# Packing W1 and W2 into seven 64-row halves in a two-branch transformer block

## The chip, the cores and the metric

The kernel runs on one core of one Trainium2 chip. The metric is device time in microseconds (us); lower is better. A run with a profile also leaves a trace, and times inside the kernel are counted from the start of the traced span. All runs told of here are in the fast state, but for two of the four runs of experiment 2, which are marked where they come. The kernel before was run again beside the experiments, on several chips, with medians of 177.70 to 178.31 us in place of 177.94; so totals of different experiments compare only within some 0.6 us.

Engine names as the profile prints them: PE is TensorE's matmuls, PEld its weight loads, DVE is VectorE, ACT is ScalarE, POOL is GpSimd, SP is the sync engine, which here only issues DMAs.

## The reference

With S = 2048 tokens, D = 448, F = 1792 and 16 heads, on xn = layernorm(x):

```python
def _B_ref(x, w1, w2, w3, w4):                 # called with x = xn
    h  = gelu(layernorm(x) @ w1)                # 448 -> 448
    c  = D // 4                                 # 112 features in each quarter
    # quarter 0 takes token t-1, quarter 1 token t+1, quarter 2 token t-2, quarter 3 token t+2
    hs = concatenate([shift(h[:, :, k*c:(k+1)*c]) ...]) @ w2
    x1 = x + hs
    return x1 + gelu(layernorm(x1) @ w3) @ w4

out = x + attention(xn) + _B_ref(xn)            # attention: linear, with softmax feature maps of +p and -p
```

## The kernel before

Everything is bf16, sums are in PSUM, TensorE's result memory. The kernel uses its banks two at a time, as bank pairs. A recorder keeps the order in which operations are written, and each engine executes its own operations strictly in that order. The line numbers in the profile are the recorder's helpers, so groups are told apart by tile names: `xnT` and `gT` are transposed activations, `w` holds w1, w2, w3 and w4, `hT` is gelu(xn W1), `wpk` and `wpq` the folded weights of K and Q, `vaug` the V values, `phik` the key features, `g_tok` the second layernorm's output before its transpose.

K = 448 does not divide by 128. The kernel therefore works with pairs of 64-row matmuls: one on partitions 0 to 63 and one on 64 to 127, into different PSUM banks, run at the same time. Such a pair is called a pair-step below. For W2 it kept four chunks of 112 features, one for each shift, so a chunk is a 64-row half and a 48-row half:

```python
def w1_pair(g, m, b):            # 512 tokens x two chunks of 112 features
    return lap_pair([banks[2 * b + k][0:CR, :] for k in range(2)],
                 lambda k, kc, lo, hi: w1[lo:hi, kc, CR * (m + k):CR * (m + k) + CR],
                 lambda k, kc, lo, hi: xnT[lo:hi, kc, 512 * g:512 * g + 512])

def w2_pair(i, b):               # token tiles i and i + 1
    def side(k, lo, hi):
        r = []
        for m in range(NM):      # four chunks; the shift is a column offset
            c0 = 2 + 128 * (i + k) - SHIFTS[m]
            r.append((banks[2 * b + k][:, 0:D], hT[lo:hi, m, c0:c0 + 128], w2[lo:hi, m, :]))
        return r
    return (lambda: row_pairs(side(0, 0, 64), side(1, 64, CR), True),
            lambda: row_pairs(side(1, 0, 64), side(0, 64, CR)))
```

After the token and W1 stage come eight attention steps, each with a K pair, a Q pair and one W2 or V pair, and then the W3/W4 stage:

```python
side = [("w", 0), ("v", 12), ("w", 2), ("w", 4), ("v", 14), ("w", 6), ("w", 8), ("w", 10)]
g_at = {2: (0,), 3: (1,), 4: (2, 3), 6: (4,), 7: (5,)}
for ps in range(8):
    ...
    if kind == "w":
        w2_out(i, 2)             # DVE: xn += W2 result
    ...
    k_norm(2 * ps)               # DVE: sum, reciprocal; POOL: multiply phik, 3.2 us
    if kind == "w" and i < 8:
        w2_norm(i)               # DVE: statistics of tiles i, i+1; POOL: scale, every 4 tiles
    for t in g_at.get(ps, ()):
        g_apply(t)               # POOL: normalise tile t
        g_T(t)                   # SP: DMA transpose into gT
# ... [cut] ...
play([A(6, 7), G(6, 7), a(0), (wl[12][0],), b(0), ...   # a(0): first W3 pair, reads gT of tiles 0 to 3
```

The softmax here doesn't subtract the row's maximum and nothing guards it: scores larger than these inputs give would overflow.

## Time and profile before

| | before |
|---|---|
| median of 4 runs | 177.94 us (177.75 to 178.07) |
| TensorE matmul busy | 170.8 us of a span of 175.9 |
| attention steps start | 31.4 us |
| W3 stage starts | 69.0 us |

First the page of the kernel before: TensorE's busy line, its row and its clock's row in the 40 slices (tenths), and the chain that ended last, by engine.

```profile
PE 170.8 (97%) x2198; PEld 94.7 (54%) x2198; DVE 110.0 (63%) x252; ACT 82.5 (47%) x92; POOL 93.7 (53%) x130
...
PE   7899999998999999999999999999999999999993
...
PEclk9999999999999999999999999999999999999999
...
PE 91%; DVE 6%; issue 1%; POOL 0%; ACT 0%; DVEq 0%
```

TensorE is busy nearly everywhere, and 91% of the chain of waits lies on it: whatever delays TensorE is paid in full.

The windows view of the kernel before gives one line for each stage: length, then busy time (and instructions) of PE, PEld, DVE, ACT and POOL, the granted clock, the DMA share and GB/s.

```profile
core 0: us, PE busy (x) PEld busy (x) DVE busy (x) ACT busy (x) POOL busy (x), PEclk, DMA share, GB/s
0.00:17.70 17.70, 15.86 (x176) 10.48 (x178) 13.92 (x39) 9.71 (x14) 10.16 (x34) 1.00 0.81 205
17.70:31.40 13.70, 13.69 (x209) 8.84 (x206) 7.87 (x20) 9.49 (x13) 5.74 (x10) 1.00 0.56 142
31.40:69.00 37.60, 37.12 (x520) 20.99 (x517) 32.01 (x54) 30.77 (x34) 26.69 (x18) 1.00 0.29 96
69.00:175.90 106.90, 104.15 (x1308) 54.42 (x1304) 56.16 (x141) 32.48 (x33) 51.09 (x70) 1.00 0.25 53
```

The third line is the eight attention steps: 37.6 us, 37.1 of them busy on TensorE. DVE (32.0) has little room in it, POOL (26.7) some.

The timeline of TensorE around the first W3 matmul of the kernel before (start, length, engine, line, operation, tiles, shapes, count; a bracket at the end would name idle time and its releaser):

```profile
68.32 0.83 PE L203 MATMUL bank<-xnT,wpq 64*128 64x512 bf16 x6
68.97 1.04 PE L203 MATMUL bank<-gT,w 64*128 64x512 bf16 x8
```

There is no bracket: the last Q matmuls run into W3. POOL's timeline shows why, in the same kernel:

```profile
58.08 3.21 POOL L215 TENSOR_TENSOR phik<-phik,rks 128x1792 bf16<-128x1792 bf16 x1
61.28 1.51 POOL L215 TENSOR_SCALAR g_tok<-xn,rs 128x512 bf16<-128x512 bf16 x2
62.76 3.21 POOL L215 TENSOR_TENSOR phik<-phik,rks 128x1792 bf16<-128x1792 bf16 x1
```

Token tiles 2 and 3 are normalised (`g_tok<-xn,rs ... x2`) by 62.8 us, between two phik multiplies of 3.21 us; their transposes had some 3 us to spare: the last was issued at 63.3 and, at the 2.4 us that such a transpose takes to land, was there at 65.7, while W3 began at 68.97.

### The profile page before, as it was taken

Reading aid. Unit: us, or ns where it says so; the run is one execution under the profiler, and the core shown is the slowest. Engines: PE = TensorE matmul, PEld = TensorE weight load, DVE = VectorE, ACT = ScalarE, POOL = GpSimd, SP = SyncE. Lnnn points to the kernel's source line nnn. Section 1 sums busy time; section 2 is a strip of 40 time slices with the busy share of each in tenths; the row PEclk is TensorE's granted clock in tenths of the full one; section 3 lists DMA queues with packets and bytes.
Section 4 is the critical chain, followed back from the end, with each engine's and each line's share of the span. In section 5 each row is a group of like instructions: output and inputs, shape, how many; then the busy total and the mean of one; then the engine's idle time right before and its main releaser. Section 6 shows DMA issues by size and latency. Waiting matters only on the chain.

```text
span 175.9 us, 5042 instructions
## 1 busy us (share of the span) xinstructions
PE 170.8 (97%) x2198; PEld 94.7 (54%) x2198; DVE 110.0 (63%) x252; ACT 82.5 (47%) x92; POOL 93.7 (53%) x130
## 2 busy tenths in 40 slices
PE   7899999998999999999999999999999999999993
PEld 4466557744565555665554554554545545545551
DVE  4799906699899697615776981644427415474621
ACT  2368874997779877926324422223214222224000
POOL 3666670016799999860358489460620723523740
PEclk9999999999999999999999999999999999999999
DMA  5994158990001120121011372134611310311331
GB/s 172 330 240 79 35 97 255 390 345 15 0 4 30 34 60 4 30 55 39 4 34 40 79 74 59 48 82 89 93 30 57 82 34 0 86 30 30 86 100 34
DMA packets 32981, 14.87 MB, mean 85 GB/s; under 512 B 24704, under 2 KB 32448, under 8 KB 32960
## 3 DMA queue, kind: packets, MB, share of 16 engines
q1 hardware_dynamic: 30192, 12.64, 29.6%
q10 hardware_dynamic: 2768, 1.92, 3.4%
q8 instruction: 17, 0.28, 0.7%
q14 instruction: 4, 0.03, 0.1%
HBM read 7.08 MB, written 1.84 MB: 51 GB/s over the span
## 4 chain that ended last, share of the span: by engine, by line
PE 91%; DVE 6%; issue 1%; POOL 0%; ACT 0%; DVEq 0%
PE bank L203 90%; DVE vaug L215 1%; DVE st L215 1%; DVE ksum L215 1%; PE bank L207 1%; DVE xn L215 1%; DVE mv L215 0%; ACT xnT L211 0%; POOL rs L215 0%; DVE rks L215 0%; DVEq L176 0%; DVE gT L215 0%; POOL mv L215 0%
## 5 line engine op out<-in xcount | busy, mean ns | idle before, releaser
L211 ACT ACTIVATE phik<-bank 128x1024 bf16<-128x1024 f32 (+1 forms) x44 | 42.3, 984 | 62.4 <-PE bank L203 62.4
L203 PE MATMUL bank<-gT,w 64*128 64x512 bf16 x392 | 50.1, 377 | 0.0
L215 DVE TENSOR_TENSOR vaug<-bank,vaug 128x464 f32<-128x464 f32 (+3 forms) x65 | 32.6, 512 | 23.0 <-PE bank L203 21.4
L203 PE MATMUL bank<-w,phik 64*128 64x448 bf16 (+1 forms) x420 | 45.0, 349 | 0.0
L215 POOL TENSOR_TENSOR xnT<-vaug 128x196 bf16<-128x196 f32 (+1 forms) x32 | 18.1, 585 | 46.8 <-DVE vaug L215 46.8
L203 PEld LDWEIGHTS bank<-w,phik 64*128 64x128 bf16 (+1 forms) x420 | 21.7, 94 | 21.2 <-issue 0.4
L215 POOL TENSOR_TENSOR phik<-phik,rks 128x1792 bf16<-128x1792 bf16 x8 | 25.7, 3212 | 10.8 <-DVE rks L215 10.8
L203 PEld LDWEIGHTS bank<-gT,w 64*128 64x128 bf16 x392 | 18.6, 94 | 17.0 <-ACT hi L211 0.3
L215 POOL TENSOR_TENSOR vaug<-xn,xtok 128x448 f32<-128x448 bf16 x16 | 16.2, 1031 | 0.2 <-DVE vaug L215 0.2
L215 DVE TENSOR_REDUCE ksum<-phik 128x64 f32<-128x1792 bf16 x8 | 16.0, 2006 | 0.0
L203 PE MATMUL bank<-w,hT 64*128 64x448 bf16 (+1 forms) x128 | 15.0, 349 | 0.5 <-DVE vaug L215 0.5
L215 DVE RECIPROCAL vaug<-bank 128x16 f32<-128x16 f32 x16 | 4.1, 257 | 18.0 <-PE bank L203 18.0
L203 PE MATMUL bank<-xnT,wpq 64*128 64x512 bf16 x112 | 14.9, 376 | 0.0
L203 PE MATMUL bank<-xnT,w 64*112 64x512 bf16 x112 | 14.8, 380 | 0.0
L203 PE MATMUL bank<-wpk,xnT 64*128 64x448 bf16 x112 | 13.4, 349 | 0.0
L203 PE MATMUL bank<-wo,xnT 64*128 64x448 bf16 (+1 forms) x106 | 13.4, 349 | 0.0
L215 DVE TENSOR_TENSOR xn<-bank,xn 128x512 bf16<-128x512 f32 (+1 forms) x16 | 9.2, 616 | 6.3 <-PE bank L203 6.3
L203 PE MATMUL bank<-wv,xnT 64*128 64x448 bf16 x112 | 13.0, 350 | 0.1
L215 POOL TENSOR_TENSOR rs<-mv,mhalf 128x1 f32<-128x1 f32 (+2 forms) x18 | 12.2, 679 | 1.5
L215 POOL TENSOR_SCALAR g_tok<-xn,rs 128x512 bf16<-128x512 bf16 x16 | 12.1, 767 | 0.2
L211 ACT ACTIVATE xnT<-bank 128x512 bf16<-128x512 bf16 x12 | 7.0, 603 | 6.3 <-PE bank L207 6.3
L215 DVE BATCH_NORM_STATS2 st<-xtok 128x6 f32<-128x448 bf16 x16 | 9.8, 615 | 0.0
(62 smaller groups left out, 168.0 us busy)
## 6 DMA issues: line engine op xcount, KB each, us to landing
w<-in_B_w_dram SPq DMA_DIRECT2D x2, 896.0 KB, 7.1
out_dram<-vaug SPq DMA_DIRECT2D x15, 112.0 KB, 1.9
w<-in_B_w_dram SPq DMA_DIRECT2D x1, 1568.0 KB, 12.0
xtok<-in_A_x_dram ACTq DMA_DIRECT2D x2, 448.0 KB, 7.3
xtok<-in_A_x_dram SPq DMA_DIRECT2D x2, 224.0 KB, 5.7
w<-in_B_w_dram ACTq DMA_DIRECT2D x2, 224.0 KB, 5.8
wo<-in_A_wo_dram SPq DMA_DIRECT2D x2, 224.0 KB, 8.4
w<-in_B_w_dram SPq DMA_DIRECT2D x1, 392.0 KB, 3.8
```

What stands on the lines that cost most here:

```text
L203: self.op("PE", lambda e: e.matmul(out, lhsT, rhs, start=start, stop=stop, skip_group_check=True), [out], [lhsT, rhs], tile=self._tile(lhsT))
L207: self.op("PE", lambda e: e.transpose(out, in_, ident), [out], [in_, ident], tile=self._tile(in_))
L211: self.op("ACT", lambda e: e.activation(out, in_, func, **kw), [out], [in_] + aps)
L215: self.op(eng, lambda e: getattr(e, name)(out, *args, **kw), [out], aps)
```

## The change

The intent: the 448 features of W2's contraction are seven halves of 64, not eight (four of 64 and four of 48), so W2 can do with 56 pair-steps of matmuls in place of 64. W1 has to deliver its output in that packing: two blocks of 128 features, one block of 128 in 256-token steps, and the last 64 features as 64x64 tiles, four at a time (a quad). Halves now mix two shifts, so the few odd rows are shifted by DMAs out and back. The last half lies with tokens 0 to 511 on the low and 512 to 1023 on the high partitions, so a W2 pair takes tiles i and i + 4. That in turn moved the statistics, the scale and the normalisation, and POOL's order. The core of the diff, cuts marked:

```diff
-        def w1_pair(g, m, b):
+        def wa_pair(g, b):     # features 0-255, 512 tokens
+        def wc_pair(g, b):     # features 256-383, 2 x 256 tokens
+        def wd_pair(h, b):     # features 384-447: 64x64 tiles, four at a time, 256 tokens each
 ... [bodies cut]
         def w2_pair(i, b):
-            def side(k, lo, hi):
-                for m in range(NM): ...
+            def side(k, j, rows):
+                t, r = i + 4 * j, []
+                for c in range(3): ...
+                if k: r.append((..., hD[lo:hi, t // 8, c0:c0 + 128], w2[lo:hi, 3, :]))
 ...
+        R.dma(w2[:, 0:3, :], ...)            # W2 is now loaded ahead of the token transposes
+        for p0 in (0, 64): R.dma(w2[p0:p0 + 64, 3, :], B_w2[384:448, :])
 ...
-        for i in range(12, NT):
+        for i in range(10, NT):              # six tiles transposed by DMA, not four
             xn_Td(i)
 ...
+        for h in range(2): hop_out(h); hop_in(h)     # shift the odd rows
+        halo()
+        load_rest()
 ...
-        side = [("w", 0), ("v", 12), ("w", 2), ("w", 4), ("v", 14), ("w", 6), ("w", 8), ("w", 10)]
-        g_at = {2: (0,), 3: (1,), 4: (2, 3), 6: (4,), 7: (5,)}
+        side = [("v", 12), ("w", 0), ("w", 1), ("w", 2), ("w", 3), ("v", 14), ("w", 8), ("w", 9)]
+        g_at = {5: (0, 1), 6: (2,), 7: (3,)}
 ...
-            k_norm(2 * ps)
-            if kind == "w" and i < 8: w2_norm(i)
+            if ps == 5: ln_scale(mv2, rs2, 0, 8, 8)
             for t in g_at.get(ps, ()): g_apply(t); g_T(t)
+            k_norm(2 * ps)
+            if kind == "w" and i < 4: ln_stats(.., i); ln_stats(.., i + 4)
```

More of the change, by code (lines that the diff above doesn't have):

```diff
@@ L84, in solve @@
         tiles = {}
-        mode = (None, 0)
         for eng, fn, w, r, dma, tile in self.ops:
@@ L113, in solve @@
             if eng == "PE":
-                if tile[1] != mode[0]:
-                    mode = (tile[1], mode[1] + 1)
                 for k in w:
                     for lo, (i, m) in tiles.setdefault(k, {}).items():
-                        if lo != tile[0] and m == mode[1]:
+                        if lo != tile[0] and m == tile[1]:
                             need["PE"] = max(need.get("PE", -1), i)
-                    tiles[k][tile[0]] = (pos["PE"], mode[1])
+                    tiles[k][tile[0]] = (pos["PE"], tile[1])
             kn = known[eng]
@@ L198, in _tile @@
         row_bytes, _ = self.rows[a.tensor.name]
-        rows = list(a.ap)[0][1]
-        return a.offset * DTB[a.dtype] // row_bytes, 128 if rows > 64 else 64
+        rows, cols = list(a.ap)[0][1], a.shape[-1]
+        return a.offset * DTB[a.dtype] // row_bytes, (rows > 64, cols > 64)
     def mm(self, out, lhsT, rhs, start, stop):
@@ L232, in bass_parallel_sum__linear_kernel_hedgehog__mixer_s_mlp__prompt_kernel @@
     CR = 112
-    SHIFTS = [1, -1, 2, -2]
-    HW = S + 16
+    SHIFTS = ((1, -1, 2), (1, -1, -2))
+    HW = S + 32
+    HB, DW = 16, 528
     x2d, out2d = A_x[0], out[0]
@@ L284, in bass_parallel_sum__linear_kernel_hedgehog__mixer_s_mlp__prompt_kernel @@
         w2 = new("w2", NM * D).rearrange("p (m d) -> p m d", m=NM)
+        hD = hT[:, 3, 0:2 * DW].rearrange("p (b s) -> p b s", b=2)
+        hop_t = [view(hi_r, 2048, at=8192), view(hi_r, 2048, at=12288), gT[:, 1, :, :].rearrange("p c s -> p (c s)")]
         wo = new("wo", KC * D).rearrange("p (c d) -> p c d", c=KC)
@@ L368, in bass_parallel_sum__linear_kernel_hedgehog__mixer_s_mlp__prompt_kernel @@
         load_wT(0)
+        R.dma(w2[:, 0:3, :], B_w2[0:384, :].rearrange("(c p) d -> p c d", p=128))
+        for p0 in (0, 64):
+            R.dma(w2[p0:p0 + 64, 3, :], B_w2[384:448, :])
         def load_rest():
-            R.dma(w2[0:CR, :, :], B_w2.rearrange("(m p) d -> p m d", p=CR))
             load_lap(w3, B_w3)
@@ L387, in bass_parallel_sum__linear_kernel_hedgehog__mixer_s_mlp__prompt_kernel @@
         R.ew(pool, "memset", mhalf[:, :], -0.5)
-        R.ew(pool, "memset", hT[:, :, 0:2], 0.0)
-        R.ew(pool, "memset", hT[:, :, S + 2:S + 4], 0.0)
+        R.ew(pool, "memset", hT[:, 0:3, 0:HB], 0.0)
+        R.ew(pool, "memset", hT[:, 0:3, S + HB:S + 2 * HB], 0.0)
+        R.ew(pool, "memset", hD[:, :, 512:DW], 0.0)
         busy = gT[:, 0, 0, 0:256]
@@ L494, in bass_parallel_sum__linear_kernel_hedgehog__mixer_s_mlp__prompt_kernel, with row_pairs @@
         LO, HI = (0, 64), (64, 128)
-        def row_pairs(first, second, start=False):
+        def row_pairs(first, second, start=False, cols=1):
             for s, (p, q) in enumerate(zip(first, second)):
-                for out, lhs, rhs in (p, q):
+                for out, lhs, rhs in (p, q) if cols == 1 else (*p, *q):
                     R.mm(out, lhs, rhs, start and s == 0, False)
@@ L528, in v_out @@
                 R.ew(dve, "tensor_copy", vd, vs)
-        def w1_pair(g, m, b):
-            return lap_pair([banks[2 * b + k][0:CR, :] for k in range(2)],
-                         lambda k, kc, lo, hi: w1[lo:hi, kc, CR * (m + k):CR * (m + k) + CR],
-                         lambda k, kc, lo, hi: xnT[lo:hi, kc, 512 * g:512 * g + 512])
-        def w1_out(g, m, b):
-            R.act(hT[0:CR, m:m + 2, 2 + 512 * g:2 + 512 * g + 512], two(2 * b)[0:CR, :, :], ACT.Gelu_apprx_tanh)
-        def w2_pair(i, b):
-            def side(k, lo, hi):
-                r = []
-                for m in range(NM):
-                    c0 = 2 + 128 * (i + k) - SHIFTS[m]
-                    r.append((banks[2 * b + k][:, 0:D], hT[lo:hi, m, c0:c0 + 128], w2[lo:hi, m, :]))
-                return r
-            return (lambda: row_pairs(side(0, 0, 64), side(1, 64, CR), True),
-                    lambda: row_pairs(side(1, 0, 64), side(0, 64, CR)))
+        def wa_pair(g, b):
+            return lap_pair([banks[2 * b + k] for k in range(2)],
+                            lambda k, kc, lo, hi: w1[lo:hi, kc, 128 * k:128 * k + 128],
+                            lambda k, kc, lo, hi: xnT[lo:hi, kc, 512 * g:512 * g + 512])
@@ new lines, in wa_out, with wc_out @@
+        def wa_out(g, b):
+            R.act(hT[:, 0:2, HB + 512 * g:HB + 512 * g + 512], two(2 * b), ACT.Gelu_apprx_tanh)
+        def wc_pair(g, b):
+            return lap_pair([banks[2 * b + k][:, 0:256] for k in range(2)],
+                            lambda k, kc, lo, hi: w1[lo:hi, kc, 256:384],
+                            lambda k, kc, lo, hi: xnT[lo:hi, kc, 512 * g + 256 * k:512 * g + 256 * k + 256])
+        def wc_out(g, b):
+            R.act(halves(hT[:, 2, HB + 512 * g:HB + 512 * g + 512]), two(2 * b)[:, :, 0:256], ACT.Gelu_apprx_tanh)
@@ new lines, in wd_pair, with side @@
+        def wd_pair(h, b):
+            def side(k, q, rows, kcs):
+                lo, hi = rows
+                t0 = 512 * (2 * h + q) + 256 * k
+                return [(banks[2 * b + k][64 * q:64 * q + 64, 0:256], w1[lo:hi, kc, 384:448], xnT[lo:hi, kc, t0:t0 + 256])
+                        for kc in kcs]
+            up, down = (0, 1, 2, 3), ((0, 1, 3), (0, 2, 3))
+            return (lambda: row_pairs([*zip(side(0, 0, LO, up), side(0, 1, LO, up))],
+                                      [*zip(side(1, 0, HI, up), side(1, 1, HI, up))], True, 2),
+                    lambda: row_pairs([*zip(side(1, 0, LO, down[0]), side(1, 1, LO, down[0]))],
+                                      [*zip(side(0, 0, HI, down[1]), side(0, 1, HI, down[1]))], False, 2))
@@ new lines, in wd_out, with hop_out, hop_in @@
+        def wd_out(h, b):
+            R.act(halves(hD[:, h, 0:512]), two(2 * b)[:, :, 0:256], ACT.Gelu_apprx_tanh)
+        MINOR = ((112, 128, 17, 15), (96, 128, 14, 17), (64, 80, 14, 18))
+        def hop_out(h):
+            for c, (p0, p1, src, dst) in enumerate(MINOR):
+                x0, x1 = ((src, HB + 1024), (HB + 1024, src + S))[h]
+                R.dma(hop_t[c][p0:p1, x0 - src:x1 - src], hT[p0:p1, c, x0:x1])
+        def hop_in(h):
+            for c, (p0, p1, src, dst) in enumerate(MINOR):
+                cut = HB + 1024 + min(0, dst - src)
+                x0, x1 = ((dst, cut), (cut, dst + S))[h]
+                R.dma(hT[p0:p1, c, x0:x1], hop_t[c][p0:p1, x0 - dst:x1 - dst])
@@ new lines, in halo @@
+        def halo():
+            for g in range(3):
+                p, q = 64 * (g % 2), 64 * ((g + 1) % 2)
+                R.dma(hD[p:p + 64, g // 2, 512:514], hD[q:q + 64, (g + 1) // 2, 0:2])
+        def w2_pair(i, b):
+            def side(k, j, rows):
+                lo, hi = rows
+                t, r = i + 4 * j, []
+                for c in range(3):
+                    c0 = HB + 128 * t - SHIFTS[lo > 0][c]
+                    r.append((banks[2 * b + j][:, 0:D], hT[lo:hi, c, c0:c0 + 128], w2[lo:hi, c, :]))
+                if k:
+                    c0 = 128 * (t % 4) + 2
+                    r.append((banks[2 * b + j][:, 0:D], hD[lo:hi, t // 8, c0:c0 + 128], w2[lo:hi, 3, :]))
+                return r
+            return (lambda: row_pairs(side(1, 0, LO), side(1, 1, HI), True),
+                    lambda: row_pairs(side(0, 1, LO), side(0, 0, HI)))
@@ L548, in w2_out @@
         def w2_out(i, b):
             for p0, p1, x0 in ((0, 256, 0), (256, D, 320)):
-                R.ew(dve, "tensor_tensor", xn[:, i:i + 2, p0:p1], two(2 * b)[:, :, p0:p1],
-                     xn[:, i:i + 2, x0:x0 + p1 - p0], op=ALU.add)
+                R.ew(dve, "tensor_tensor", xn[:, i:i + 5:4, p0:p1], two(2 * b)[:, :, p0:p1],
+                     xn[:, i:i + 5:4, x0:x0 + p1 - p0], op=ALU.add)
         def k_exp(i, b, s):
@@ L722, in bass_parallel_sum__linear_kernel_hedgehog__mixer_s_mlp__prompt_kernel @@
             ln1_stats(i, 1, 0)
-            if i not in (0, 4):
+            if i:
                 ln1_apply(dve, i - 1)
-            if i == 3:
-                ln1_apply(dve, 3)
         phi_blocks()
@@ L734, in bass_parallel_sum__linear_kernel_hedgehog__mixer_s_mlp__prompt_kernel, with WA, WC, WD @@
         ln1_stats(14, 1, 0)
-        ln1_apply(dve, 12)
-        ln1_apply(dve, 13)
         ln1_stats(15, 1, 0)
-        ln1_apply(dve, 14)
-        ln1_apply(dve, 15)
         for i in range(12, NT):
+            ln1_apply(dve, i)
+        for i in range(10, NT):
             xn_Td(i)
-        load_rest()
         late_3()
-        vps = {i: v_pair(i, b) for i, b in ((0, 2), (2, 3), (4, 3), (6, 2), (8, 2), (10, 3))}
-        wps = {(g, m): w1_pair(g, m, b) for g, m, b in ((0, 0, 0), (0, 2, 1), (1, 0, 0), (1, 2, 1), (2, 0, 0),
-                                                        (2, 2, 1), (3, 0, 0), (3, 2, 2))}
-        fps = {(t, m): fold_pair(t, m, b) for t, m, b in ((1, 0, 2), (1, 2, 3), (0, 0, 1), (0, 2, 3))}
+        vps = {i: v_pair(i, b) for i, b in ((0, 2), (2, 3), (4, 3), (6, 2), (8, 1), (10, 1))}
+        was = {g: wa_pair(g, b) for g, b in ((0, 0), (1, 0), (2, 3), (3, 2))}
+        wcs = {g: wc_pair(g, b) for g, b in ((0, 1), (1, 3), (2, 1), (3, 1))}
+        wds = {h: wd_pair(h, b) for h, b in ((0, 2), (1, 3))}
+        fps = {(t, m): fold_pair(t, m, b) for t, m, b in ((1, 0, 0), (1, 2, 2), (0, 0, 0), (0, 2, 2))}
         def V(i, k):
             return (vps[i][k],)
-        def W(g, m, k):
-            return (wps[g, m][k],)
+        def WA(g, k):
+            return (was[g][k],)
+        def WC(g, k):
+            return (wcs[g][k],)
+        def WD(h, k):
+            return (wds[h][k],)
         def FO(t, m, k):
@@ L760, in bass_parallel_sum__linear_kernel_hedgehog__mixer_s_mlp__prompt_kernel @@
         play([(xn_T, 0, 0), (spin, 3, 256), (xn_T, 1, 1), (spin, 4, 256), V(0, 0), (xn_T, 2, 0), V(0, 1), (xn_T, 3, 1),
-              (spin, 2, 256), V(2, 0), (v_out, 0, 2), W(0, 0, 0), (xn_T, 4, 2), V(2, 1), (v_out, 2, 3),
-              W(0, 2, 0), (xn_T, 5, 2), W(0, 0, 1), (xn_T, 6, 3), W(0, 2, 1), (xn_T, 7, 2), (w1_out, 0, 0, 0),
-              (w1_out, 0, 2, 1), V(4, 0), V(6, 0), V(4, 1), (v_out, 4, 3), V(6, 1), (v_out, 6, 2),
-              W(1, 0, 0), (xn_T, 8, 3, 2), W(1, 2, 0), W(1, 0, 1), (xn_T, 10, 3, 2), W(1, 2, 1),
-              (w1_out, 1, 0, 0), (w1_out, 1, 2, 1), V(8, 0), V(10, 0), V(8, 1), (v_out, 8, 2), V(10, 1),
-              (v_out, 10, 3), W(2, 0, 0), W(2, 2, 0), FO(1, 0, 0), W(2, 0, 1), (w1_out, 2, 0, 0), FO(1, 0, 1),
-              FO(1, 2, 0), W(2, 2, 1), (w1_out, 2, 2, 1), FO(1, 2, 1), W(3, 0, 0), FO(0, 0, 0), W(3, 2, 0),
-              FO(0, 0, 1), FO(0, 2, 0), W(3, 2, 1), (w1_out, 3, 2, 2), W(3, 0, 1), (w1_out, 3, 0, 0), FO(0, 2, 1)])
+              (spin, 2, 256), V(2, 0), (v_out, 0, 2), WA(0, 0), (xn_T, 4, 2), V(2, 1), (v_out, 2, 3), WA(0, 1),
+              (xn_T, 5, 2), WC(0, 0), (xn_T, 6, 3), WC(0, 1), (xn_T, 7, 2), (wa_out, 0, 0), (wc_out, 0, 1),
+              V(4, 0), V(6, 0), V(4, 1), (v_out, 4, 3), V(6, 1), (v_out, 6, 2),
+              WA(1, 0), (xn_T, 8, 1, 2), WC(1, 0), WA(1, 1), (wa_out, 1, 0), WC(1, 1), (wc_out, 1, 3),
+              WD(0, 0), V(8, 0), WD(0, 1), (wd_out, 0, 2), V(8, 1), (v_out, 8, 1),
+              FO(1, 0, 0), WA(2, 0), FO(1, 0, 1), FO(1, 2, 0), WA(2, 1), (wa_out, 2, 3), FO(1, 2, 1),
+              V(10, 0), FO(0, 0, 0), V(10, 1), (v_out, 10, 1), FO(0, 0, 1), FO(0, 2, 0), WC(2, 0), FO(0, 2, 1),
+              WC(2, 1), (wc_out, 2, 1),
+              WA(3, 0), WD(1, 0), WA(3, 1), (wa_out, 3, 2), WD(1, 1), (wd_out, 1, 3), WC(3, 0), WC(3, 1), (wc_out, 3, 1)])
+        for h in range(2):
+            hop_out(h)
+            hop_in(h)
+        halo()
+        load_rest()
         def w2_norm(i):
@@ L787, in bass_parallel_sum__linear_kernel_hedgehog__mixer_s_mlp__prompt_kernel @@
                 kv_tile(2 * ps - 5)
-            w[0]()
+            if ps:
+                w[0]()
+            else:
+                q[0]()
             k[1]()
@@ L791, in bass_parallel_sum__linear_kernel_hedgehog__mixer_s_mlp__prompt_kernel @@
                 k_exp(2 * ps, 1, s)
-            q[0]()
+            if ps:
+                q[0]()
+            else:
+                w[0]()
+                q[1]()
             w[1]()
@@ L797, in bass_parallel_sum__linear_kernel_hedgehog__mixer_s_mlp__prompt_kernel @@
                 v_out(i, 2, "DVE" if i == 12 else "ACT")
-            q[1]()
+            if ps:
+                q[1]()
             for s in range(2):
                 q_exp(2 * ps, 0, s)
-            k_norm(2 * ps)
-            if kind == "w" and i < 8:
-                w2_norm(i)
+            if ps == 5:
+                ln_scale(mv2, rs2, 0, 8, 8)
             for t in g_at.get(ps, ()):
@@ L806, in bass_parallel_sum__linear_kernel_hedgehog__mixer_s_mlp__prompt_kernel @@
                 g_T(t)
+            k_norm(2 * ps)
+            if kind == "w" and i < 4:
+                ln_stats(st2, mv2, xn, i)
+                ln_stats(st2, mv2, xn, i + 4)
         w3p = [w3_pair(p) for p in range(28)]
         fp = [fin_pair(2 * k) for k in range(7)]
-        wl = {i: w2_pair(i, 2) for i in (12, 14)}
+        wl = {i: w2_pair(i, 2) for i in (10, 11)}
         def a(p):
@@ L840, in bass_parallel_sum__linear_kernel_hedgehog__mixer_s_mlp__prompt_kernel @@
         play([
-            A(6, 7), G(6, 7),
-            a(0), (wl[12][0],), b(0), a(1), (w2_last, 12), b(1), K(10, 11, 12, 13),
-            a(2), (wl[14][0],), b(2), a(3), K(14, 15), b(3), (kv_copy,),
-            a(4), (w2_last, 14), b(4), a(5), (kv_blocks,), b(5),
+            A(4, 5, 6, 7), G(4, 5, 6, 7),
+            a(0), (wl[10][0],), b(0), a(1), (w2_last, 10), b(1), K(10, 11, 12, 13),
+            a(2), (wl[11][0],), b(2), a(3), K(14, 15), b(3), (kv_copy,),
+            a(4), (w2_last, 11), b(4), a(5), (kv_blocks,), b(5),
             a(6), N(0), (w2_norm, 8), b(6), a(7), f(1, 0), b(7), N(1), (w2_norm, 10), A(8, 9, 10, 11),
```

## The prediction

> **What bounds the kernel now.** TensorE. The busy table gives it 170.8 of 175.9 us; the chain of waits gives it 91% of the span. By the timeline, the token/W1 stage lasts to 31.4 us, eight attention steps follow (K, Q and one W2 or V pair each, about 4.8 us a step) to 69.0 us, then the W3/W4 stage runs on TensorE without gaps to 173 us. A pair of row-packed matmuls costs about 216 ns at 512 columns and 191 ns at 448.
>
> **What the change removes.** W2 goes from 64 pair-steps to 56: 8 x 0.19 = 1.5 us. W1 goes from 56 pair-steps of 512 (12.1 us) to 28 of 512 (6.05), 28 of 256 (about 3.1) and 14 quads of 64x64 tiles. Two token tiles' PE transposes go to DMA (0.2 us saved). The Trainium skill ("TensorEngine Tiling (Array Packing)", Restrictions) says that column tiling excludes Fast Weight Load; the trace has no 64-column load, but its 112-column loads take 127 ns against 94 ns for 128 columns. Estimate from that: a quad about 0.2 us, plus mode switches. So W1 gains nothing: 12 to 12.7 us. Six serial DMA transposes (1.27 us each) may make the fourth W1 group wait 0.5 us. The attention steps start at about 31.8 us.
>
> **What it moves, which decides.** W2 pairs four apart mean that tiles 0 to 3 are all normalised only after the step-4 pair. In before the four tiles' transposes had landed by about 65 us, 4 us before the W3 stage began. Now:
> - VectorE: four W2 steps in a row cost 5.02 us each (residual add 1.07, reduce and reciprocal 2.5, statistics 1.4, measured start to start), against 4.65 us of TensorE, so TensorE waits about 1 us over these steps, and 0.5 us for the V copy before them.
> - POOL runs in program order: phik multiply (8), scale chain 1.6 us, token tiles 0 and 1 (0.77 each), multiply (10) 3.21 us, tile 2, multiply (12) 3.21 us, tile 3, then its DMA transpose 2.4 us. Counted from the start of step 5, multiply (8) ends at about 7, tile 3 is on POOL's way out at about 18 and lands at 20 to 21, while TensorE finishes step 7 at about 14.
> - So the first W3 matmul waits about 6.5 us, and TensorE, in order, has nothing else. Its start goes from 69.0 to about 75.5 us. Nothing later has slack to give this back.
>
> The idle stretch also costs clock. The Trainium skill ("TensorE: Matmul & The Clock Gate", Part 1) says that an idle window of about 3.4 us returns the array to half rate. The trace agrees for a cold start: the first 19 matmuls of 256 columns took 4.07 us, median 418 ns, later ones 272 ns. Estimate: 1.8 us more. The two W2 pairs left in the last stage save 0.4 us.
>
> **Sum.** 178.0 + 6.5 + 1.8 - 0.4 = 185.9 us. Predicted 185.5, range 181.5 to 188.5. Chances: faster by over 2% 0.05, within 2% 0.09, slower by over 2% 0.86.
>
> **What would show it.** TensorE idle of 5 to 7 us just before the first gT-reading W3 matmul, released by the DMA transpose of token tile 3; POOL's tile-3 apply after the multiply (12), well past step 7's last matmul; longer matmuls for 3 to 4 us after it; attention steps of about 5.0 us in the W2 run; matmul busy of W2 down by about 1.5 us; W1 in all about unchanged.
>
> **What would make it wrong.** POOL reaching tile 3 earlier than its program order allows me to count (then about 177 us); the clock not dropping (184 us); quads loading weights in parallel (1.3 us less); shift DMAs landing late (more).

## The result, and the profile after

The changed kernel takes 190.52 us (median of 4 runs, 190.15 to 190.73) against 177.94: the ratio is 1.0706, with a 95% interval of 1.0686 to 1.0726. Ratios here and below are the mean time of one kernel's fast runs over that of the other's of the same rounds, so they are not quite the ratio of the medians quoted.

The same lines of the page, for the changed kernel:

```profile
PE 171.7 (91%) x2222; PEld 90.2 (48%) x2222; DVE 110.2 (58%) x252; ACT 81.1 (43%) x92; POOL 93.6 (50%) x128
...
PE   7899886899999994099999999999999999999994
...
PEclk9999999999999999669999999999999999999999
...
PE 64%; DVE 20%; POOL 6%; DMA 6%; issue 1%; ACT 1%; ACTq 0%; DVEq 0%
```

TensorE is idle in two places that were full: the fifth to eighth slices (8, 8, 6, 8), and the sixteenth and seventeenth (4, 0). The clock's row falls to 6 in the two slices from the seventeenth on. The chain lies on TensorE for only 64% of the span.

The windows of the changed kernel, cut where its own stages end (columns as above):

```profile
0.00:17.40 17.40, 15.33 (x178) 9.55 (x180) 14.47 (x41) 9.31 (x14) 11.07 (x35) 1.00 0.89 213
17.40:35.40 18.00, 14.37 (x251) 8.32 (x248) 9.23 (x28) 10.09 (x15) 5.69 (x11) 1.00 0.50 87
35.40:72.70 37.30, 36.40 (x496) 18.32 (x496) 30.28 (x45) 29.21 (x32) 22.61 (x11) 1.00 0.38 121
72.70:80.20 7.50, 0.19 (x2) 0.01 (x1) 3.21 (x4) 3.22 (x3) 7.50 (x5) 0.78 0.17 35
80.20:188.40 108.20, 105.44 (x1302) 53.99 (x1302) 53.01 (x137) 29.28 (x30) 46.75 (x69) 0.98 0.28 53
```

Set beside the windows of before, the traced span's 12.5 us divide like this:

| stage | before | after | difference |
|---|---|---|---|
| until the attention steps | 31.4 | 35.4 | +4.0 |
| eight attention steps | 37.6 | 37.3 | -0.3 |
| wait for W3 | 0 | 7.5 | +7.5 |
| from the first W3 matmul | 106.9 | 108.2 | +1.3 |

TensorE around the first W3 matmul of the changed kernel:

```profile
72.08 0.81 PE L200 MATMUL bank<-xnT,wpq 64*128 64x512 bf16 x6
80.22 1.89 PE L200 MATMUL bank<-gT,w 64*128 64x512 bf16 x8 [7.33 <-DMA gT<-g_tok]
81.88 1.72 PE L200 MATMUL bank<-w,hT 64*128 64x448 bf16 x8
```

It waited 7.33 us for the DMA transpose that fills `gT`. The eight matmuls that took 1.04 us before took 1.89: the array came back at half rate. Cut into windows of 0.6 us, the granted clock is at half from about 76.8 us, 4 us after the last Q matmul, to about 83.6. POOL's timeline shows what the transpose waited for:

```profile
62.59 3.22 POOL L212 TENSOR_TENSOR phik<-phik,rks 128x1792 bf16<-128x1792 bf16 x1 [1.77 <-DVE rks L212]
65.89 0.22 POOL L212 TENSOR_SCALAR mv<-mv 128x8 f32<-128x8 f32 x1
66.19 1.66 POOL L212 TENSOR_TENSOR rs<-mv,mhalf 128x8 f32<-128x8 f32 x1
67.94 0.21 POOL L212 TENSOR_SCALAR rs<-mv 128x8 f32<-128x8 f32 x1
68.26 1.53 POOL L212 TENSOR_SCALAR g_tok<-xn,rs 128x512 bf16<-128x512 bf16 x2
69.75 3.21 POOL L212 TENSOR_TENSOR phik<-phik,rks 128x1792 bf16<-128x1792 bf16 x1
72.94 0.77 POOL L212 TENSOR_SCALAR g_tok<-xn,rs 128x512 bf16<-128x512 bf16 x1
73.68 3.21 POOL L212 TENSOR_TENSOR phik<-phik,rks 128x1792 bf16<-128x1792 bf16 x1
76.87 0.77 POOL L212 TENSOR_SCALAR g_tok<-xn,rs 128x512 bf16<-128x512 bf16 x1
```

Read it downwards: the multiply of step 4 (the "multiply (8)" of the prediction) ends at 65.8, the scale chain takes until 68.2, tiles 0 and 1 until 69.8, then a multiply, tile 2, a multiply, and only at 76.87 tile 3. Before, tile 3 was done at 62.8.

The waits of TensorE in the changed kernel (who waited for whom: us in total, times, longest):

```profile
PE bank L200 <- DMA gT<-g_tok: 7.3, 1, 7.3
...
PE bank L200 <- DVE wpq L212: 1.5, 1, 1.5
...
PE bank L200 <- ACT vaug L208: 0.7, 1, 0.7
...
PE bank L200 <- ACT hT L208: 0.7, 1, 0.7
PE bank L200 <- DMA xnT<-xn: 0.7, 1, 0.7
```

The first line is the W3 wait. The other four, 3.6 us in all, lie in the W1 stage: for the copies of the folded Q weights (`wpq`), for a V copy and a gelu that still read a PSUM bank pair, and for a token transpose (`xnT`). TensorE's matmul busy time up to the attention steps hardly changed, 29.55 us before (15.86 + 13.69) and 29.70 after (15.33 + 14.37); its idle time in that stage rose from 1.85 to 5.70 us.

The 1.50 us that the view gives to `wpq` need care. The fourth W1 group starts at 30.79; the copies ended at 30.2, while the last token transpose, issued at 26.02, landed 4.6 us later, at about 30.6. In the traces of experiments 3 and 5 the same wait is put down to that transpose. So the group waited for both, and the copies alone would have let it go about half a microsecond earlier.

### The profile page after: what moved, and what is told of

The parts are those of the page before. It is cut to its first block, busy times and chain, and to the rows that moved or that the text cites. A ratio compares the mean times of both kernels' runs of the same rounds, so it can differ in the third digit from the quotient of the medians.

```text
span 188.4 us, 5107 instructions
## 1 busy us (share of the span) xinstructions
PE 171.7 (91%) x2222; PEld 90.2 (48%) x2222; DVE 110.2 (58%) x252; ACT 81.1 (43%) x92; POOL 93.6 (50%) x128
## 3 DMA queue, kind: packets, MB, share of 16 engines
q10 hardware_dynamic: 2768, 1.92, 3.2%
## 4 chain that ended last, share of the span: by engine, by line
PE 64%; DVE 20%; POOL 6%; DMA 6%; issue 1%; ACT 1%; ACTq 0%; DVEq 0%
PE bank L200 64%; DVE st L212 6%; DVE ksum L212 5%; DVE xn L212 4%; POOL phik L212 3%; DMA xtok<-in_A_x_dram 3%; DMA xnT<-xn 2%; DVE mv L212 2%; POOL g_tok L212 2%; DMA gT<-g_tok 1%; DVE rks L212 1%; POOL rs L212 1%; DVE vaug L212 1%; DVE wpq L212 1%; ACT vaug L208 0%
## 5 line engine op out<-in xcount | busy, mean ns | idle before, releaser
L200 PE MATMUL bank<-gT,w 64*128 64x512 bf16 x392 | 51.0, 382 | 7.3 <-DMA gT<-g_tok 7.3
L200 PE MATMUL bank<-xnT,w 64*128 64x256 bf16 (+2 forms) x168 | 13.7, 308 | 2.9 <-DVE wpq L212 1.5
L212 POOL TENSOR_TENSOR vaug<-xn,xtok 128x448 f32<-128x448 bf16 x16 | 16.2, 1034 | 0.2 <-DVE vaug L212 0.2
L200 PE MATMUL bank<-w,hT 64*128 64x448 bf16 x112 | 14.1, 366 | 0.7 <-DVE vaug L212 0.4
L212 DVE RECIPROCAL vaug<-bank 128x16 f32<-128x16 f32 x16 | 4.1, 257 | 17.9 <-PE bank L200 17.9
L200 PE MATMUL bank<-wv,xnT 64*128 64x448 bf16 x112 | 13.6, 351 | 0.5 <-ACT xnT L208 0.2
L212 POOL TENSOR_TENSOR rs<-mv,mhalf 128x1 f32<-128x1 f32 (+3 forms) x17 | 12.0, 707 | 1.4
L208 ACT ACTIVATE hT<-bank 128x512 bf16<-128x512 f32 (+1 forms) x10 | 7.3, 767 | 7.1 <-PE bank L200 7.1
L200 PEld LDWEIGHTS bank<-xnT,w 64*128 64x128 bf16 (+1 forms) x168 | 6.5, 98 | 7.5 <-DVE wpq L212 1.7
## 6 DMA issues: line engine op xcount, KB each, us to landing
w<-in_B_w_dram SPq DMA_DIRECT2D x1, 1568.0 KB, 10.2
```

What stands on the lines that cost most here:

```text
L200: self.op("PE", lambda e: e.matmul(out, lhsT, rhs, start=start, stop=stop, skip_group_check=True), [out], [lhsT, rhs], tile=self._tile(lhsT))
L208: self.op("ACT", lambda e: e.activation(out, in_, func, **kw), [out], [in_] + aps)
L212: self.op(eng, lambda e: getattr(e, name)(out, *args, **kw), [out], aps)
```

## The experiments

Every kernel passed the check of its result, even the one of experiment 7, whose result is wrong: so the check does not see that error. "W1 stage" below ends where the attention steps start, 31.4 us before and 35.4 after.

### 1. POOL's order alone, in the kernel before (b_g_late)

```diff
-        g_at = {2: (0,), 3: (1,), 4: (2, 3), 6: (4,), 7: (5,)}
+        g_at = {5: (0, 1), 6: (2,), 7: (3,)}        # and ahead of k_norm, as in the change
-            A(6, 7), G(6, 7),
+            A(4, 5, 6, 7), G(4, 5, 6, 7),
```

> The kernel before, with only the POOL order of the change: token tiles 0 and 1 normalised in step 5, 2 in step 6, 3 in step 7, each ahead of that step's phik multiply, the rest as before. Theory (order alone makes the wait): TensorE waits about 5.8 us before the first W3 matmul, and with the clock loss the run takes about 185 us. Rival (the wait comes of W2's pairs four apart or of the DMA shifts): 178 us, no wait.

Measured: 185.97 us (185.02 to 186.74), ratio 1.0460 (1.0421 to 1.0500). TensorE waited 5.72 us for the transpose into `gT`. TensorE's first W3 matmuls, and POOL's timeline, in this kernel:

```profile
74.76 1.89 PE L203 MATMUL bank<-gT,w 64*128 64x512 bf16 x8 [5.72 <-DMA gT<-g_tok]
...
67.43 0.77 POOL L215 TENSOR_SCALAR g_tok<-xn,rs 128x512 bf16<-128x512 bf16 x1
68.16 3.21 POOL L215 TENSOR_TENSOR phik<-phik,rks 128x1792 bf16<-128x1792 bf16 x1
71.36 0.77 POOL L215 TENSOR_SCALAR g_tok<-xn,rs 128x512 bf16<-128x512 bf16 x1
```

Neither packing nor pairs four apart are in this kernel, and it loses 8 us. Tile 3 sits behind the multiply of 3.21 us exactly as in the change. The rival falls. (The edit also moves the applies of tiles 4 and 5 into the last stage, as the change does.)

### 2. The same order put right in the changed kernel (a_g_first)

```diff
-        g_at = {5: (0, 1), 6: (2,), 7: (3,)}
+        g_at = {5: (0, 1, 2, 3)}
```

> The changed kernel, with the four normalisations of token tiles 0 to 3 all put on POOL straight after the scale chain in step 5, ahead of the phik multiplies (10) and (12). Theory (POOL's program order makes the first W3 matmul wait, and the idle stretch costs clock): the normalisations end at about 71.3 us in place of 77.6, the four DMA transposes follow at 1.27 us each and the last lands at about 75.2, so TensorE waits about 2.5 us in place of 7.3 and the clock does not drop: about 184.4 us. Rival (the packed W1 and W2 matmuls and their mode switches are the cost): no gain, 190.5 us.

Measured: two fast runs of 187.54 and 184.92 us; the other two, 187.97 and 189.33, count as slow (over 1.5% above the fastest), so no ratio could be given. In the run of 184.92, close to the 184.4 expected, the mean clock was 1.00. The traced run is the one of 187.54 (mean clock 0.98). In its trace the wait before W3 is 2.94 us in place of 7.33, close to the 2.5 expected; the four transposes, 1.27 us each to issue, are what is left. But the W1 stage of this run ended at 37.16 us, 1.8 later than in the changed kernel, with the clock down. Its windows:

```profile
29.00:31.00 2.00, 0.37 (x8) 0.11 (x6) 1.48 (x8) 0.60 (x1) 0.00 (x0) 1.00 0.24 50
31.00:33.00 2.00, 2.00 (x12) 0.65 (x16) 0.00 (x0) 0.00 (x0) 0.00 (x0) 0.50 0.21 49
```

The granted clock is 0.50 after a token-transpose wait of 1.63 us that followed other short waits. And the matmuls after the W3 wait slowed again: the first eight still took 1.04 us, and half rate set in 1.2 us after work had resumed (78.8 to 82.2 us). So that part of the expectation was wrong for this run: 2.9 us of idling was enough. The mechanism is confirmed; the total is met by one of two fast runs.

### 3. Filling the wait with work: the clock's share (a_spin, then b_g_late_2 and b_late_spin)

```diff
+        def filler(n):
+            for _ in range(n):
+                R.mm(banks[3][:, 0:256], ident[:, 0:128], w4[:, 0, 0:256], True, True)
-            a(0), (wl[10][0],), b(0),
+            (filler, 60), a(0), (wl[10][0],), b(0),
```

> The changed kernel with 60 idle-work matmuls of 256 columns (about 6.6 us, into a bank that is then overwritten) put in TensorE's queue just before the first W3 matmul. Theory (about 1.3 to 1.8 us of the loss is the clock that drops in the 7.3 us of idling): the W3 stage starts at the same time, its first matmuls run at full rate, and the run takes about 189.0 us in place of 190.5. Rival (the clock term is nothing, the loss is the wait alone): 190.5 us.

Measured: 191.22 us (190.35 to 192.91), not the 189.0 expected. The clock held at 1.0, and from the first W3 matmul to the end it took 106.6 us in place of 108.2, the expected gain. But W3 started at 82.05 in place of 80.22: the W1 stage was 0.7 us longer in the traced run, and the last transpose took 3.63 us to land in place of 2.41. As a total this run settles nothing, so the test was repeated as a pair in the kernel of experiment 1, whose W1 stage is that of before.

> The kernel before with POOL's order of the change, once more, as the partner of the next run on the same chip: about 186 us, a wait of 5.7 us before the first W3 matmul, and some 3 us of half-rate matmuls after it.

> The same with 48 matmuls of 256 columns (about 5.3 us of work whose result is overwritten) ahead of the first W3 matmul, in a kernel whose W1 stage has no waits that scatter. Theory (the idling costs clock beside time): W3 starts at the same time, no half-rate matmuls follow, and the run is 1.3 to 1.8 us faster than its partner. Rival (the clock term is nothing, or the fill work costs what it saves): the same time as its partner.

Measured: 186.09 us (185.35 to 186.35) without and 184.05 us (183.93 to 184.16) with 48 filling matmuls, on the same chip. TensorE's timeline without, and then with them:

```profile
69.16 0.83 PE L203 MATMUL bank<-xnT,wpq 64*128 64x512 bf16 x6
75.61 1.89 PE L203 MATMUL bank<-gT,w 64*128 64x512 bf16 x8 [5.62 <-DMA gT<-g_tok]
```

```profile
69.49 5.41 PE L203 MATMUL bank<-w,ident 128*128 128x256 bf16 x48
75.29 1.04 PE L203 MATMUL bank<-gT,w 64*128 64x512 bf16 x8 [0.39 <-DMA gT<-g_tok]
```

W3 starts within 0.3 us of the same time in both, but its first eight matmuls take 1.89 us after the idling and 1.04 after the filler. Idling cost 2.0 us of clock (186.09 - 184.05), 0.3 of which is the earlier start.

### 4. Only three bank pairs exchanged in the W1 stage (a_banks)

```diff
-        was = ... (3, 2)    wcs = ... (3, 1)    wds = ... (1, 3)
+        was = ... (3, 3)    wcs = ... (3, 0)    wds = ... (1, 2)
```

> The changed kernel with only three PSUM bank pairs of the W1 stage exchanged: the fourth group of W1 takes the pair that has long been read, its 64-column part the pair of the Q-weight fold, and its last part the pair that the first K step doesn't need. Theory (the 4 us that the W1 stage lost are waits for bank pairs, not matmul time): the waits of 1.50 us (for the copies of the folded Q weights) and of 0.69 us (for the last gelu) go, the attention steps start at about 33.3 us in place of 35.4, and the run takes about 188.4 us. Rival (column-tiled matmuls and mode switches made the stage long): the attention steps still start at 35 us and the run takes 190.5 us.

Measured: 190.32 us (188.69 to 190.70), so the total did not follow. The stage became shorter. TensorE's timeline of this kernel, from the third W1 group to the attention steps:

```profile
24.57 1.04 PE L200 MATMUL bank<-xnT,w 64*128 64x512 bf16 x8 [1.92 <-issue]
...
29.95 4.47 PE L200 MATMUL bank<-xnT,w 64*128 64x256 bf16 x62
34.26 0.92 PE L200 MATMUL bank<-wpk,xnT 64*128 64x448 bf16 x8
```

From the third W1 group to the first K matmul it took 9.69 us; in the changed kernel it took 11.99 (23.41 to 35.40). Not all of the 2.3 us are bank waits: the third group started 1.2 us later here, so the last token transpose had landed (at 30.4) before the fourth group needed it (30.5). A fairer partner is the kernel of experiment 7, which has the old bank pairs and a third group as late, at 24.83, with the last transpose landed before the fourth group: it took 11.45 us. So the bank pairs exchanged here are worth about 1.8 us, and about 0.5 is the transpose's. The wait of 0.72 us for the V copy was not touched by the exchange and is still there.

In the total the gain was lost again. The wait at 24.57 was 1.92 us in place of 0.66 (the view names no releaser for it; in the other runs the same wait is for the token transpose), and from the first W3 matmul it took 109.4 us in place of 108.2. In the windows the clock is at half from 74.6 to 84.8 us, 10.2 us, against 6.8 in the changed kernel and 3.4 for each of the two stretches of experiment 2: one, two and three times 3.4. The 12 half-rate stretches found in the traces after the first 20 us, cut into such intervals, all ended with the first one through which TensorE worked (but for 0.2 us at most). Here the first W3 matmul came at 79.15, 1.1 us into the second interval (78.0 to 81.4), so a third followed; in the changed kernel it came at 80.22, where the second began. This fits every trace, but no experiment tested it.

### 5. W2's load moved behind the token transposes (a_w2_after)

```diff
-        R.dma(w2[:, 0:3, :], ...); ...       # right after the Q and K weights' transposes
         for i in range(10, NT):
             xn_Td(i)
+        R.dma(w2[:, 0:3, :], ...); ...
```

> The changed kernel with the three loads of W2 issued after the six token transposes in the sync engine's queue, not ahead of them. Theory (the wait of 0.7 to 2.0 us before the third W1 group is its token transposes queued behind these loads, which take 1.8 us to issue): that wait is gone, the attention steps start at about 34.7 us, and the run takes about 189.5 us, with 1 us of scatter for the clock. Rival (the transposes are late because the DMA engines are busy): the wait stays.

Measured: 190.07 us (190.01 to 190.73). The wait before the third W1 group is gone (it started at 22.79, 0.6 us earlier, with no wait), and the attention steps start at 34.94. The expected reason, queueing behind three loads that take 1.8 us to issue, does not come out of this pair of runs: the first token transpose began to issue at 18.45 us in the changed kernel and at 18.57 here, because the weights' transposes ahead of both ended at 16.2 there and at 18.0 here. What differs is the second transpose, 2.3 us to issue there and 1.6 here. Against the kernel of experiment 7, whose sync queue was as late as here (17.9), the loads do show: its token transposes began at 19.79, and its third group waited 2.05 us where this one did not wait. So the loads cost about 1.2 us in that pair; their issue time was not told apart from their traffic. The total moved by only 0.45 us. The next wait, at the fourth group, became the DMA's own: 1.65 us for the transpose of the last token tiles.

### 6. All known waits out of the W1 stage (a_w1_fixed)

```diff
+        # W2 load after the transposes; tokens 10, 11 transposed on TensorE again;
+        # bank pairs: was (3, 1), wcs (2, 3), (3, 2), wds (1, 0)
```

> The changed kernel with every wait taken out of the W1 stage and nothing else: W2 loads after the token transposes, tokens 10 and 11 transposed on TensorE as before, and bank pairs chosen so that none is still being read. Theory (the W1 stage's 4 us are waits; the packed matmuls themselves cost about what the old ones did): the attention steps start at 31.5 to 32.2 us, the wait before the first W3 matmul stays at 7.3 us, and the run takes about 187 us. Rival (the packed matmuls are slower): the attention steps start after 34 us.

Measured: 189.11 us (188.50 to 189.72), ratio 1.0613. The attention steps start at 33.69 us, 1.7 earlier than in the change but 1.5 later than hoped: a wait of 0.62 us for a copy of the two new transposes and one of 0.99 us for the last DMA transpose had taken the place of the others. This lies between what the theory and its rival expected, and settles for neither. The W3 wait stayed at 7.3 us, as expected.

### 7. Without the shift DMAs: a wrong result (a_no_hops)

```diff
-        for h in range(2):
-            hop_out(h)
-            hop_in(h)
-        halo()
```

> Wrong result on purpose: the changed kernel without the DMAs that shift the 16 or 32 odd rows of each mixed half and without the halo copies. Theory (these DMAs are off every critical wait): 190.5 us, within 0.5. Rival (shift DMAs that land late, or that hold back the loads of W3 and W4 and the token transposes behind them, cost time): over 1 us faster.

Measured: 191.67 us (191.17 to 193.14): no faster, rather 1 us slower, and outside what was expected. In its trace the token-transpose wait at the third W1 group, which lies before any shift DMA, was 2.05 us, within the scatter seen elsewhere. The shift DMAs cost the change nothing that shows in the total. In the W1 stage they may cost up to 0.5 us: from the third group to the first K matmul it took 11.45 us here and 11.99 in the change, and the last token transpose landed 3.5 us after its issue in place of 4.6.

### 8. Attention steps reordered (a_att_fixed), and both repairs (a_both_fixed)

```diff
-        side = [("v", 12), ("w", 0), ("w", 1), ("w", 2), ("w", 3), ("v", 14), ("w", 8), ("w", 9)]
+        side = [("w", 0), ("w", 1), ("v", 12), ("w", 2), ("w", 3), ("v", 14), ("w", 8), ("w", 9)]
+            if kind == "v": ln_stats of four tiles            # in the V steps
+            if ps in (3, 6): ln_scale and g_apply of two tiles, ahead of k_norm
```

> The changed kernel with the attention steps alone reordered: W2 pairs in steps 0, 1, 3, 4 and V pairs in 2 and 5, both V copies on ScalarE, statistics moved into the V steps, tiles 0 and 1 scaled and normalised in step 3 and tiles 2 and 3 in step 6, each ahead of that step's phik multiply. Theory: no wait before the first W3 matmul, no dropped clock there, steps of about 4.65 us, about 180.3 us; what is left over 178 is the W1 stage. Rival (packed W2 is itself slow, or waits return elsewhere): above 184 us.

> Both repairs together: the packed matmuls of the change with neither the waits of the W1 stage nor the one before W3. Theory: 31.8 us for the W1 stage, 36.3 for the eight steps, then the last stage less 0.4: about 176.7 us, that is 0.5 to 0.9% faster than before, which is all that the seven halves are worth. Rival (the packing costs as much as it saves): 178 us or more.

Measured: 187.08 us (186.31 to 189.01) and 183.92 us (183.13 to 184.34). Both expectations failed by the same mistake: TensorE still waited 4.1 and 3.95 us before W3. POOL's timeline of the second:

```profile
65.10 3.21 POOL L212 TENSOR_TENSOR phik<-phik,rks 128x1792 bf16<-128x1792 bf16 x1 [0.97 <-DVE rks L212]
68.41 0.19 POOL L212 TENSOR_SCALAR mv<-mv 128x2 f32<-128x2 f32 x1
...
69.78 1.53 POOL L212 TENSOR_SCALAR g_tok<-xn,rs 128x512 bf16<-128x512 bf16 x2
```

I had put the scale of tiles 2 and 3 one step too late: in program order it follows a multiply that itself waited for its sums. It is the mistake of the change, made again at a smaller size. In a_att_fixed the W1 stage also ran to 38.33 us, after a token-transpose wait of 2.51 us that took the clock to 0.54.

### 9. The repair mended (best1, best2)

```diff
+            if kind == "v": ln_stats, then ln_scale and g_apply of two tiles, then k_norm   # best1
+        ln1_apply(dve, 12); ln1_apply(dve, 13)     # order of the first layernorm as before
+            if ps == 7: ln_scale(mv2, rs2, 4, 4, 4); g_apply(4); g_T(4)   # best2: ahead of k_norm
```

> Both repairs, mended after the last runs showed that scaling of tiles 2 and 3 still sat behind a phik multiply and that tokens 12 to 15 were normalised late: scale and normalisation now stand in the V steps ahead of that step's multiply, the first-layer normalisation has its old order, and in step 0 K's second half comes ahead of W2. Theory: no wait before W3, attention steps start at about 32.3 us, eight steps of 36.3 us, last stage 106.5: about 177.0 us, 0.5% faster than before. Rival (the packing costs as much as it saves): 178 us or more.

> The last repaired version with one thing more: token tile 4 is scaled and normalised on POOL in step 7 ahead of the phik multiply (14), which had left the transposes of tiles 4 to 7 late and TensorE waiting 1.34 us at the eighth W3 pair. Theory: that wait goes, 176.6 us, 0.8 to 1.0% faster than before. Rival (the multiply (14), now 2.3 us later, holds up the K-V product instead): 177.9 us, no gain.

Measured: best1 177.90 us (177.23 to 178.09), ratio 0.9978 (0.9961 to 0.9995), with a wait of 1.34 us left in the W3 stage. best2, without it, 176.99 us (176.50 to 177.53) against 178.19 for the kernel before in the same rounds: ratio 0.9927 (0.9901 to 0.9952). The windows of best2, attention steps and the rest:

```profile
32.45:68.62 36.17, 36.11 (x500) 18.12 (x496) 29.62 (x45) 30.82 (x35) 25.88 (x18) 1.00 0.49 136
68.62:175.40 106.78, 103.97 (x1304) 52.91 (x1301) 56.20 (x141) 32.48 (x33) 52.58 (x73) 1.00 0.25 53
```

The steps take 36.17 us, 1.4 less than before, and TensorE is busy in 36.11 of them. This version is 0.7% faster than the kernel before (interval 0.5 to 1.0%) and 7% faster than the change. Both versions also contain the edits of experiment 6 and a new order of the first attention step, with V copies on ACT. That order was not tried in the kernel before, so how much of the gain is packing is not shown.

### 10. The column-tiled block computed twice (best1_wd_twice)

```diff
-  WD(1, 1), (wd_out, 1, 0), WC(3, 0), WC(3, 1),
+  WD(1, 1), WC(3, 0), WD(1, 0), WC(3, 1), WD(1, 1), (wd_out, 1, 0),
```

> The same with the second column-tiled W1 block (7 quads of 64x64 tiles in two segments) computed twice, the second time from a cleared bank, so the result is right. Theory: a quad costs about 0.11 us and a change of tile shape about 0.15 to 0.2 us, so this adds 1.2 to 1.5 us to the run. Rival (my prediction's 0.2 us for a quad): at least 1.9 us. Rival (quads cost the streaming of 256 columns alone): 0.8 us.

Measured in the trace: from the same point of the W1 stage to the first K matmul, 5.06 us (28.09 to 33.15) against 4.07 in best1 (28.06 to 32.13). So seven quads in two segments cost 1.0 us, about 0.14 each with the changes of tile shape, between the theory and the third guess. Start to start the trace shows quads 0.11 us apart, which leaves about 0.1 us for each segment's changes of shape. The total moved by only 0.5 us (178.37 against 177.90), because best1's later wait of 1.34 us shrank to 0.3.

## Why the prediction was right or wrong

The direction and the mechanism were right: the prediction named the POOL chain, the tile and the place. The size was wrong: 185.5 predicted, at most 188.5, and 190.52 measured. Term by term, in the traced span:

- **W1 stage, "The attention steps start at about 31.8 us": this step failed.** They started at 35.4, 3.6 us later; that is most of the 4.6 us by which the sum (185.9) missed. The matmul time was rightly held to be unchanged (29.55 and 29.70 us); what grew is TensorE's idle time, from 1.85 to 5.70 us. For it the prediction had one transpose wait of 0.5 us, at the fourth group. It had no term for the PSUM bank pairs: a matmul group waits until the engine that reads the pair's former content is done, and the new schedule reused pairs just after a copy had been given to DVE or ACT. Experiment 4 changed three such pairs and the stretch shrank by 2.3 us, about 1.8 of it the bank pairs' (against experiment 7's kernel); a wait of 0.72 us for the V copy comes on top. The token transposes were sized too low: 0.66 us at the third group, and about 0.5 more at the fourth. This is shown in the stage; the totals of experiments 4 and 5 hardly moved. The bank pairs could have been read from the diff: pair 2 serves the Q fold (four DVE copies, 1.28 us) and then the fourth W1 group.
- **The W3 wait, "about 6.5 us": right, a little low.** It was 7.3 to 7.5. Experiment 1 shows that order alone makes a wait of 5.7 us, in the kernel before; experiment 2, that 7.3 become 2.9 once the two multiplies are out of the way.
- **"four W2 steps in a row cost 5.02 us each": right.** The residual adds after the four W2 steps start 4.98 to 5.02 us apart (43.89, 48.91, 53.89 and 58.88 in VectorE's timeline of the changed kernel), and the eight steps took 37.3 us where W2's saving alone (six steps of 0.19) would have made them about 36.5.
- **Clock, "1.8 us more": right.** The pair in experiment 3 gives 2.0, less 0.3 for an earlier start; the changed kernel's last stage, 1.3 us longer although W2 saves 0.4 there, gives the same 1.7; experiment 3's filler in the changed kernel, 1.6. The Trainium skill ("TensorE: Matmul & The Clock Gate", Part 1) says that an idle window of about 3.4 us brings half rate, and the trace agrees, 1.89 us for matmuls that take 1.04. But it happened after shorter gaps too: in experiment 2 after one of 2.94 us, and after one of 1.63 us that followed one of 0.72.
- **"a quad about 0.2 us": wrong in size, without weight.** It is 0.14 us. The Trainium skill ("TensorEngine Tiling (Array Packing)", Restrictions) does say that column tiling excludes Fast Weight Load, and I made slow loads of that. In the trace a 64x64 load is indeed the slower one, 106 ns against 94 for 64x128, by the last figure before the second bar:

```profile
L200 PEld LDWEIGHTS bank<-xnT,w 64*128 64x128 bf16 x112 | 5.3, 94 | 6.1 <-DVE wpq L212 1.7 <-ACT vaug L208 0.9 <-ACT hT L208 0.8
...
L200 PEld LDWEIGHTS bank<-xnT,w 64*64 64x64 bf16 x56 | 1.2, 106 | 1.4 <-issue 1.2 <-ACT xnT L208 0.2
```

But the 56 loads together kept the weight path busy for only 1.2 us, so about five ran at a time (56 x 106 ns in 1.2 us), against two of the 64x128 ones (112 x 94 ns in 5.3 us). That is the prediction's own way to be wrong, "quads loading weights in parallel".

What the packing is worth was as predicted in kind. Six of W2's eight pairs lie in the attention steps, which should save 1.1 us there. In experiment 9 TensorE's busy time over these steps falls by 1.0 us (37.12 to 36.11), and the steps by 1.4; the other 0.4 is idle time, which the new order took away. W1's packing brings no gain: best2's attention steps start at 32.45 us, 1.0 later than before. Of that, best1 and best2 show 0.5 us of waits for ScalarE copies; the rest was not traced.

Two things stay open. That half rate begins and ends in intervals of 3.4 us (experiment 4) is read from the traces and was not tested. And the wait at the third W1 group varies from 0.66 to 2.51 us between kernels whose queues are the same up to there. That lateness comes from further up the sync engine's queue: the weights' transposes, ahead of the tokens', begin at 5.45 us in the changed kernel and at 6.09 to 6.88 in the runs of experiments 2, 3, 4, 7 and 8. What delays those was not traced.

## What to carry to other kernels

When a change moves work on an engine that is "only half busy", walk that engine's program order to the next thing the bound engine needs, with the measured length of everything in front of it: here TensorE waited 7.3 us with two multiplies of 3.2 us ahead of the last normalisation, and 2.9 without them, while the best repaired version gained 1.2 us on the kernel before, not all of it by packing. Do the same for each PSUM pair: list who reads it last and when, before giving it to the next group. And count a wait of a few us on TensorE with the clock that follows it.

## What the Trainium skill lacked or had wrong

- "TensorE: Matmul & The Clock Gate", Part 1, ties the fall to half rate to an idle window of about 3.4 us. Here a gap of 2.51 us, and one of 1.63 us that followed one of 0.72, were followed by a granted clock of 0.54 and 0.50, while gaps of 2.05 and 1.81 us in other runs were not: a gap well under the window is not safe. Where the gap lies seems to decide (read from the traces, not tested). In the 3.4 us before half rate set in, TensorE had been busy for 1.0 us (the gap of 2.51) and 1.2 us (the one of 1.63). In the trace with the gap of 2.05, intervals of 3.4 us counted back from its later half-rate stretch split the gap. The same part tells of a kernel whose frequent short idling made the clock go up and down, without saying how long the gaps were. Filling a gap of 5.6 us with 5.4 us of dummy matmuls made the run 2.0 us faster (186.09 to 184.05), 0.3 of it by an earlier start.
- "TensorEngine Tiling (Array Packing)", Key Properties, says that changing the tiling mode drains the array, without a cost. Here seven quads in two segments, with their changes of shape, took 1.0 us; quads start 0.11 us apart within a segment, so about 0.1 us is left for each segment (an estimate). The page's Restrictions, on Fast Weight Load, do not say how long a column-tiled load takes: here 106 ns for 64x64 against 94 ns for 64x128, with about five running at a time, so that it cost no time that shows.
- "DMA: Bandwidth & Descriptors", DMA Transpose (X-bar), gives no time for issuing or landing a transpose of one token tile: on the sync engine's queue each took about 1.27 us to issue in the median, back to back (single ones up to 2.3), and 2.4 to 4.7 us to land. The one time in the skill for a DMA transpose is on another page, for a 128x128 block.
